# A spectral filter and a Gelu feed-forward block on one core: where the filter tables come from, and when batch 1 is transformed

## The chip, the cores and the metric

The kernel runs on one core of a Trainium2 chip. The metric is the device time of one execution in microseconds; before the change it is 802.97 us, the median of three runs (802.93 to 803.73). The profile is one execution, with a span of 798.2 us.

The engines are named as in the profile: PE is TensorE (matmuls; PEld are its weight loads), DVE is VectorE, ACT is ScalarE, POOL is GpSimd, SP is SyncE, whose queue issues transfers. SBUF is the memory beside the engines, with 128 partitions; PSUM holds the results of matmuls, and DRAM is outside the core.

## The reference

`x` has 8 batches of 3008 positions with 256 channels. Along the positions it is transformed (a real Fourier transform), multiplied with a complex filter for each frequency and channel, and transformed back. The result goes through a feed-forward block with an exact Gelu:

```python
X = np.fft.rfft(x, axis=1)                 # x: (8, 3008, 256)
F = (filt_r + 1j * filt_i)[None, :, :]     # (1505, 256), two real tables
y = np.fft.irfft(X * F, n=3008, axis=1)
h = y.reshape(24064, 256) @ w_in           # (256, 2048)
g = 0.5 * h * (1 + erf(h / sqrt(2)))
out = g @ w_out                            # (2048, 256)
```

Inputs and output are float32; the kernel works in bfloat16 with float32 sums.

## The kernel before

3008 is 47 x 64, and the transform is done in two steps by matmuls with small tables: T1 over the 47, T2 over the 64; then the filter, then T3 and T4 back. Batches 1 to 7 go through four kinds of units: `s1` (first step, 16 units of one matmul, line 233), `s2` (second step and filter, 12 units, line 256), `s3` (back, 12 units, line 280), `s4` (back, 16 units, line 307). Between `s1` and `s2`, and between `s3` and `s4`, the data must change their layout, which they do by being written to DRAM (`R1`, `R2`) and read back (`r1`, `r2`). Batch 0 has nothing to hide behind, and is done in its own way without DRAM (`c1`, `c1t`, `c2`, `c3`, `c3t`), with transposes on PE.

The filters lie in `F`: both tables, 24 rows of 256 channels, in four groups of 32 partitions. Groups 0 and 1 hold a direct and a mirrored reading of the table; groups 2 and 3 hold the same again, for the other half of each complex product. Before the change the lower half is read from DRAM (with a cast from float32) and the upper half is copied from it:

```python
    def load_filters(self, k0, k):
        nc, D = self.nc, self.D
        for t, src in enumerate((self.filt_r, self.filt_i)):
            direct = _dram(src, k0 * D, [[NA * D, 32], [D, k], [1, D]])
            mirror = _dram(src, (NA - k0) * D, [[NA * D, 32], [-D, k], [1, D]])
            for q, a in enumerate((direct, mirror)):
                nc.gpsimd.dma_start(out=self.F[32 * q:32 * q + 32, t, k0:k0 + k, :], in_=a)
        nc.sync.dma_start(out=self.F[64:128, :, k0:k0 + k, :], in_=self.F[0:64, :, k0:k0 + k, :])
```

The filter product of batch 0; a step `p` uses rows 2p and 2p+1 of F:

```python
    def c2(self, p):
        # ...
        for t, o, n in ((p1, 1, 0), (p2, 0, 1)):
            # ... two matmuls (line 350) with T2[:, k, o:o + 2] into ps
            nc.vector.tensor_tensor(out=t, in0=ps, op=ALU.mult,                    # line 353
                                    in1=self.F[:, n, 2 * p:2 * p + 2, :].rearrange("p a b -> p (a b)"))
```

The table T2 has three parts: 1 and 2 come from Sin activations on ScalarE, and part 0, which only `c2` of batch 0 uses, is the negative of part 2 (the sign copy). At the end of `table_2_sin`:

```python
        act(out=self.T2[:, :, 2, 32:64], in_=self.a2[:, :, 32:64], func=AF.Sin, scale=2.0 * PI, bias=self.hm)
        self.nc.vector.tensor_scalar(out=self.T2[:, :, 0, :], in0=self.T2[:, :, 2, :], scalar1=-1.0, scalar2=None,
                                     op0=ALU.mult)
```

The order of the start-up, cut:

```python
    # ... x of batch 0 in 8 loads, tables T1 and T2
    for k in range(0, K1, 6):
        m.load_filters(k, 6)
    m.load_w_in()
    for u in range(16):
        m.c1(u // 2, u % 2)
        if u == 8:
            m.table_2_sin()
    m.load_x(1)
    m.load_w_out(0)
    m.load_w_out(8)
    m.tables_inverse()           # T3, T4 by matmuls, cast by ScalarE and VectorE
    warm = g.tile([128, 1], FP32, name="warm")
    nc.scalar.activation(out=warm, in_=m.p, func=AF.Gelu)    # loads the Gelu table
    for p in range(14):
        if p < 12:
            m.c1t(p)             # transpose, copied out by ScalarE (line 340)
        if 1 <= p < 13:
            m.c2(p - 1)
        if p in (3, 5, 7, 9, 11, 13):
            m.c3((p - 3) // 2)
    # ... c3t and s4 of batch 0
```

After that the kernel is a row of slots. In slot s, `mm1` makes one of 16 column blocks of the hidden layer for 512 tokens (two matmuls, line 408, and a Gelu on ScalarE, line 411), and from slot 16 on `mm2` makes a quarter of an output tile (four matmuls, line 422). The units of the next batch are put into slots; `s1, n1` give the slot of the first unit and the slots from one to the next, and so on. `s3` follows `s2` by 4 slots. The tokens of batch 1 are needed from slot 80:

```python
    for b in range(1, B):
        hi = first(b)            # (b * S // 512) * 16
        if b == 1:
            s1, n1, r1, s2, n2, r2, s4, n4 = 0, 0.5, 8, 17, 3.2, 58, 66, 0.8
        else:
            s1, n1, r1, s2, n2, r2, s4, n4 = hi - 94, 1, hi - 78, hi - 69, 3.7, hi - 23, hi - 17, 1
        for u in range(16):
            put(s1 + int(u * n1), m.s1, b, u)
            put(s4 + int(u * n4), m.s4, b, u // 2, u % 2)
        for c in range(4):
            put(r1, m.r1, b, c)
            put(r2, m.r2, b, c)
        for p in range(12):
            put(s2 + int(n2 * p), m.s2, b, p)
            put(s2 + int(n2 * p) + 4, m.s3, b, p)
        # ... loads of the batch after it
```

Of the kernel before, what the change touches and what calls it, by code (L numbers as in the profile page):

```python
# [9 lines left out]
AF = mybir.ActivationFunctionType  # L10
ALU = mybir.AluOpType
# [7 lines left out]
K1 = 24  # L19
# [5 lines left out]
def _dram(src, off, dims):  # L25
    return dataclasses.replace(src, offset=src.offset + off, ap=[list(d) for d in dims])


class _Mix:
# [59 lines left out]
    def load_filters(self, k0, k):  # L89
        nc, D = self.nc, self.D  # L90
        for t, src in enumerate((self.filt_r, self.filt_i)):
            direct = _dram(src, k0 * D, [[NA * D, 32], [D, k], [1, D]])
            mirror = _dram(src, (NA - k0) * D, [[NA * D, 32], [-D, k], [1, D]])
            for q, a in enumerate((direct, mirror)):
                nc.gpsimd.dma_start(out=self.F[32 * q:32 * q + 32, t, k0:k0 + k, :], in_=a)
        nc.sync.dma_start(out=self.F[64:128, :, k0:k0 + k, :], in_=self.F[0:64, :, k0:k0 + k, :])

    def gate(self, t):

# [80 lines left out]
    def table_2_sin(self):  # L180
        act = self.nc.scalar.activation
        act(out=self.T2[:, :, 1, :], in_=self.w2, func=AF.Sin, scale=2.0 * PI)
        act(out=self.T2[:, :, 2, 0:32], in_=self.a2[:, :, 0:32], func=AF.Sin, scale=-2.0 * PI, bias=self.hp)
        act(out=self.T2[:, :, 2, 32:64], in_=self.a2[:, :, 32:64], func=AF.Sin, scale=2.0 * PI, bias=self.hm)
        self.nc.vector.tensor_scalar(out=self.T2[:, :, 0, :], in0=self.T2[:, :, 2, :], scalar1=-1.0, scalar2=None,
                                     op0=ALU.mult)

    def tables_inverse(self):

        nc = self.nc  # L190
        for t4, t1, wt in ((self.T4, self.T1p, self.wt), (self.T4c, self.T1q, self.wtc)):
            ps = self.bank("ps_t4", wide=True)
            nc.tensor.matmul(ps[0:96, 0:2 * NA], lhsT=t1.rearrange("p a b c -> p (a b c)"),
                             rhs=self.eye[0:2 * NA, 0:2 * NA], start=True, stop=True)
            nc.vector.tensor_scalar(out=t4.rearrange("p n h -> p h n"),
                                    in0=ps[0:96, 0:2 * NA].rearrange("p (h n) -> p h n", h=2),
                                    scalar1=wt[0:96], scalar2=None, op0=ALU.mult)
        for q in range(6):
            ps = self.bank("ps_t3", wide=True)
            for i in range(4):  # L200
                nc.tensor.matmul(ps[:, 128 * i:128 * i + 128],
                                 lhsT=self.T2[:, 4 * q + i, 1:3].rearrange("p a b -> p (a b)"),
                                 rhs=self.eye, start=True, stop=True)

            self._evac(self.T3[:, 4 * q:4 * q + 4], ps.rearrange("p (k n r) -> p k r n", k=4, r=2), True)
# [225 lines left out]
@with_exitstack  # L431
def kernel(
    ctx: ExitStack,
    tc: tile.TileContext,
    x: bass.AP,
    filt_r: bass.AP,
    filt_i: bass.AP,
    moe_w_in: bass.AP,
    moe_w_out: bass.AP,
    out: bass.AP,  # L440
):
    m = _Mix(ctx, tc, x, filt_r, filt_i, moe_w_in, moe_w_out, out)
    nc, B, S = tc.nc, m.B, m.S
    NT = B * S // TCH
    ctx.enter_context(tc.manual_schedule())

    g = m.small
    m.p = m.iota(g, "p", [128, 1], [[0, 1]], cm=1)
    m.load_x(0, 0, 1)
    m.table_1(g)  # L450
    m.T1c = g.tile([2 * NA, 96], BF16, name="T1c")
    nc.vector.tensor_copy(out=m.T1c.rearrange("p (k h r) -> p k h r", h=2, r=2),
                          in_=m.T1.rearrange("p (h r k) -> p k h r", h=2, r=2))
    m.load_x(0, 1, 2)
    m.pi = m.iota(g, "pi", [128, 1], [[0, 1]], cm=1, dt=I32)
    m.kap = m.py.tile([128, K1, 2 * NB], FP32, tag="y", name="kap")[:, :, 0:NB]
    for sgn, lo in ((1, 0), (-1, 32)):
        nc.gpsimd.iota(m.kap[:, :, lo:lo + 32], pattern=[[1, K1], [sgn * NA, 32]], base=min(0, sgn * NA),
                       channel_multiplier=0, allow_small_or_imprecise_dtypes=True)
    m.table_2(g)  # L460
    m.load_x(0, 2, 4)
    cols = m.iota(g, "cols", [128, 128], [[1, 128]])
    m.eye = g.tile([128, 128], BF16, name="eye")
    nc.vector.tensor_scalar(out=m.eye, in0=cols, scalar1=m.p, scalar2=None, op0=ALU.is_equal)
    m.T1p = g.tile([2 * NA, 2, K1, 2], BF16, name="T1p")
    nc.vector.tensor_copy(out=m.T1p, in_=m.T1.rearrange("p (h r k) -> p h k r", h=2, r=2))
    m.T1q = g.tile([2 * NA, K1, 2, 2], BF16, name="T1q")
    nc.vector.tensor_copy(out=m.T1q, in_=m.T1.rearrange("p (h r k) -> p k r h", h=2, r=2))
    for k in range(0, K1, 6):
        m.load_filters(k, 6)  # L470
    m.load_w_in()


# [6 lines that stand above are left out]
    m.load_w_out(8)  # L480
    m.tables_inverse()
    warm = g.tile([128, 1], FP32, name="warm")
    nc.scalar.activation(out=warm, in_=m.p, func=AF.Gelu)
    for p in range(14):
        if p < 12:
            m.c1t(p)
        if 1 <= p < 13:
            m.c2(p - 1)
        if p in (3, 5, 7, 9, 11, 13):
            m.c3((p - 3) // 2)  # L490
    for u in range(20):
        if u < 16:
            m.c3t(u)
        if u >= 3 and u % 2 == 1 and (u - 3) // 2 < 8:
            for h in range(2):
                m.s4(0, (u - 3) // 2, h, both=True)


    at = {}

    def put(slot, f, *a):
        at.setdefault(slot, []).append((f, a))

    def first(b):
        return (b * S // TCH) * 16

    for b in range(1, B):
        hi = first(b)
        if b == 1:
            s1, n1, r1, s2, n2, r2, s4, n4 = 0, 0.5, 8, 17, 3.2, 58, 66, 0.8  # L510
        else:
            s1, n1, r1, s2, n2, r2, s4, n4 = hi - 94, 1, hi - 78, hi - 69, 3.7, hi - 23, hi - 17, 1
        for u in range(16):
# [8 lines that stand above are left out]
        if b + 1 < B:  # L522
            for i in range(8):
                put(s2 + int(n2 * (i + 2)), m.load_next, b, i + 2, i // 2, i % 2)

    for s in range((NT + 1) * 16):
        t, jc = s // 16, s % 16
        for f, a in at.pop(s, ()):
            f(*a)
        if t >= 1:  # L530
            m.mm2(t - 1, jc)
        if t < NT:
            m.mm1(t, jc)
    assert not at
# [30 lines left out]
```

## Time and profile before

| What | Value |
|---|---|
| time, median of three runs | 802.97 us |
| span of the profiled run | 798.2 us |
| PE busy | 767.3 us, 96% |
| ACT busy | 569.6 us, 71% |
| DVE busy | 406.4 us, 51% |
| `mm1`, one Gelu (line 411) | 752 of 597 ns |
| casts of `s1` (line 220, a_sb) | 112 of 684 ns |
| filter copies inside SBUF | 4 of 384 KB, 7.8 us to landing (median) |
| filter loads from DRAM | 16 of 96 KB as written, 5.9 us to landing (median) |

Durations of single instructions overlap with those of the next one on the same engine, so a row of Gelus runs at a shorter interval than 597 ns. Busy shares are averages over stages that have different limits; what counts for a change in one stage is which wait ends last there. The profile's views that are used below are the chain that ended last (in order of time), the timeline (instructions in order, with idle time and what ended it in brackets), and the busy time by stretches.

### The profile page before, as it was taken

The numbers are of one execution on the slowest core, as the hardware profiler recorded it, in microseconds if no ns is written. First come the engines' busy times: TensorE is split into PE (matmuls) and PEld (weight loads), VectorE is DVE, ScalarE is ACT, GpSimd is POOL, SyncE is SP. The second block draws the span as 40 slices with busy tenths as digits, with TensorE's granted clock in tenths as the row PEclk, the third lists the DMA queues.
The fourth block names the chain that finished last, engine by engine and source line by source line (L and its number), as shares of the span: only waits on it lengthen the run. The fifth ranks groups of instructions, "written<-read, shape, count | busy, mean of one in ns | idle before, by whom it ended". The sixth has DMA issues, their size and how long they took to land.

```text
span 798.2 us, 14871 instructions
## 1 busy us (share of the span) xinstructions
PE 767.3 (96%) x5950; PEld 547.5 (69%) x6042; DVE 406.4 (51%) x733; ACT 569.6 (71%) x982; POOL 56.6 (7%) x145
## 2 busy tenths in 40 slices
PE   4788999999999999999999999999999999999998
PEld 4654767667676766767677676777667776676666
DVE  6793745466453764546456464555645366420111
ACT  6667975598656885578855887558865689566663
POOL 8300200011000110002000020001100000000000
PEclk9999999999999999999999999999999999999999
DMA  8953761546425554345534466154661512401111
GB/s 140 234 100 106 147 160 47 158 109 125 128 69 156 107 104 134 77 154 109 132 85 109 139 130 146 46 134 124 118 153 54 172 62 72 133 27 40 41 41 53
DMA packets 86918, 87.23 MB, mean 109 GB/s; under 512 B 5888, under 2 KB 76544, under 8 KB 86848
## 3 DMA queue, kind: packets, MB, share of 16 engines
q1 hardware_dynamic: 78336, 70.27, 30.7%
q0 software_dynamic: 8512, 16.00, 13.8%
q8 instruction: 47, 0.77, 0.4%
q14 instruction: 23, 0.19, 0.1%
HBM read 54.00 MB, written 46.66 MB: 126 GB/s over the span
## 4 chain that ended last, share of the span: by engine, by line
PE 89%; DMA 5%; DVE 3%; issue 1%; POOL 1%; ACT 0%; SPq 0%; DVEq 0%; POOLq 0%
PE ps_o L422 41%; PE ps_h L408 37%; PE ps_s L307 3%; PE ps_s L233 3%; PE ps_s L256 2%; PE ps_s L280 2%; DMA d_sb<-R 2%; DMA x_sb<-in_x_dram 2%; DVE a_sb L220 1%; DVE d_sb L220 1%; POOL x_sb L87 1%; DVE p L353 0%; DMA b_sb<-R 0%; DVE y_sb L222 0%; DMA R<-a_sb 0%
## 5 line engine op out<-in xcount | busy, mean ns | idle before, releaser
L411 ACT ACTIVATE g_sb<-ps_h 128x512 bf16<-128x512 f32 x752 | 438.5, 597 | 194.7 <-PE ps_h L408 171.2
L422 PE MATMUL ps_o<-w_out_sb,g_sb 128*128 128x256 bf16 x3008 | 449.9, 273 | 2.6
L408 PE MATMUL ps_h<-y_sb,w_in_sb 128*128 128x512 bf16 (+7 forms) x1636 | 427.9, 350 | 0.1
L422 PEld LDWEIGHTS <-g_sb 128*128 128x128 bf16 x3008 | 287.9, 98 | 128.7 <-issue 0.6
L408 PEld LDWEIGHTS <-w_in_sb 128*128 128x128 bf16 x1728 | 165.0, 98 | 29.8 <-issue 3.9
L426 DVE COPY ost<-ps_o 128x512 f32<-128x512 f32 x94 | 64.3, 684 | 122.4 <-PE ps_o L422 121.9
L263 DVE TENSOR_TENSOR p<-ps_s,F 128x512 bf16<-128x512 f32 x84 | 58.1, 692 | 115.1 <-ACT p L262 109.0
L222 DVE TENSOR_SCALAR y_sb<-ps_s 128x376 bf16<-128x376 f32 x120 | 65.4, 547 | 81.6 <-PE ps_s L307 81.5
L220 DVE CAST a_sb<-ps_s 96x512 bf16<-96x512 f32 x112 | 75.5, 684 | 40.9 <-PE ps_s L233 40.9
L220 DVE CAST v_sb<-ps_s 128x512 bf16<-128x512 f32 x84 | 57.6, 686 | 13.0 <-PE ps_s L280 13.0
L307 PEld LDWEIGHTS <-d_sb 96*128 96x128 bf16 x512 | 34.0, 97 | 30.8 <-DMA d_sb<-R 3.9
L261 ACT ACTIVATE p<-ps_s 64x512 bf16<-64x512 f32 x84 | 49.8, 593 | 5.3 <-PE ps_s L256 3.3
L262 ACT CAST p<-ps_s 64x512 bf16<-64x512 f32 x84 | 48.5, 577 | 1.0
L233 PE MATMUL ps_s<-x_sb,T 94*96 94x512 bf16 x112 | 42.7, 383 | 1.3 <-DVE a_sb L220 1.0
L101 POOL COPY gate<-p 1x1 bf16<-1x1 bf16 x48 | 8.5, 176 | 494.4 <-DVE p L265 494.4
L307 PE MATMUL ps_s<-T,d_sb 96*128 96x94 bf16 x448 | 36.6, 204 | 2.7 <-DMA d_sb<-R 1.5
L265 DVE TENSOR_TENSOR p<-p,p 128x512 bf16<-128x512 bf16 x84 | 35.7, 425 | 2.9
L256 PE MATMUL ps_s<-b_sb,T 128*128 128x256 bf16 x168 | 32.1, 273 | 4.0 <-DMA b_sb<-R 3.6
L87 POOL DMA_DIRECT2D x_sb<-in_x_dram x64 | 33.8, 530 | 20.9 <-issue 11.6
L264 DVE TENSOR_TENSOR p<-p,F 128x512 bf16<-128x512 bf16 x84 | 34.9, 415 | 0.0
L280 PE MATMUL ps_s<-p,T 128*128 128x256 bf16 x168 | 32.1, 273 | 0.4
L280 PEld LDWEIGHTS <-T 128*128 128x128 bf16 x168 | 16.4, 98 | 19.8
(84 smaller groups left out, 182.6 us busy)
## 6 DMA issues: line engine op xcount, KB each, us to landing
out_dram<-ost SPq DMA_DIRECT2D x94, 256.0 KB, 2.5
x_sb<-in_x_dram POOLq DMA_DIRECT2D x64, 188.0 KB, 4.0
R<-a_sb SPq DMA_DIRECT2D x56, 192.0 KB, 3.0
b_sb<-R SPq DMA_DIRECT2D x28, 384.0 KB, 4.3
R<-v_sb SPq DMA_DIRECT2D x42, 256.0 KB, 4.0
d_sb<-R SPq DMA_DIRECT2D x56, 192.0 KB, 4.5
F<-F SPq DMA_DIRECT2D x4, 384.0 KB, 7.8
w_in_sb<-in_moe_w_in_dram POOLq DMA_DIRECT2D x2, 512.0 KB, 10.1
```

What stands on the lines that cost most here:

```text
L220: self.nc.vector.tensor_copy(out=out, in_=in_)
L222: self.nc.vector.tensor_scalar(out=out, in0=in_, scalar1=scale, scalar2=None, op0=ALU.mult)
L233: nc.tensor.matmul(ps[0:96, :], lhsT=self.T1, rhs=self.st[b, "x"][:, 2 * u:2 * u + 2, :], start=True, stop=True)
L261: nc.scalar.activation(out=p2[0:64], in_=ps[64:128], func=AF.Copy, scale=-1.0)
L262: nc.scalar.copy(out=p2[64:128], in_=ps[0:64])
L263: nc.vector.tensor_tensor(out=p1, in0=ps, in1=f(0), op=ALU.mult)
L280: nc.tensor.matmul(ps[:, 256 * i:256 * i + 256], lhsT=self.T3[:, k].rearrange("p a b -> p (a b)"), rhs=w[:, 256 * i:256 * i + 256], start= ...
L307: nc.tensor.matmul(ps[:, 94 * i:94 * i + 94], lhsT=d[:, (grp % 2) * 4 + i, 128 * half:128 * half + 128], rhs=t4, start=True, stop=True)
L408: nc.tensor.matmul(ps[:, o:o + n], lhsT=self.w_in_sb[:, dc, jc * 128:jc * 128 + 128], rhs=self.y[b][:, dc, off:off + n], start=(dc == 0), ...
L411: nc.scalar.activation(out=self.st["g", t][:, jc, :], in_=ps, func=AF.Gelu)
L422: nc.tensor.matmul(ps[:, tile_i % 2, :], lhsT=g[:, jc, tile_i * 128:tile_i * 128 + 128], rhs=self.w_out_sb[:, jc, :], start=(jc == 0), sto ...
L426: nc.vector.tensor_copy(out=ost, in_=ps)
```

## The change

It has four parts. (1) Both halves of F are read from DRAM, so the copy inside SBUF goes; a part is then complete as soon as its loads have landed, instead of after loads and copy. (2) The parts have 4, 6, 6 and 8 rows instead of 6 each, so that the first one is small. (3) The Gelu table is loaded in the course of the batch 0 steps instead of ahead of them, and the sign copy stands after the casts of the first step on VectorE instead of between them. (4) The units of batch 1 are placed anew: one `s1` unit in each slot instead of two in each of the first eight, the read `r1` at slot 16 instead of 8, the first `s2` at slot 26 instead of 17 with 2.8 slots between them instead of 3.2, `r2` at 61 and `s4` from 68.

```diff
-            for q, a in enumerate((direct, mirror)):
+            for q, a in enumerate((direct, mirror, direct, mirror)):
                 nc.gpsimd.dma_start(out=self.F[32 * q:32 * q + 32, t, k0:k0 + k, :], in_=a)
-        nc.sync.dma_start(out=self.F[64:128, :, k0:k0 + k, :], in_=self.F[0:64, :, k0:k0 + k, :])
@@ table_2_sin, tables_inverse
-        self.nc.vector.tensor_scalar(out=self.T2[:, :, 0, :], in0=self.T2[:, :, 2, :], scalar1=-1.0, scalar2=None,
-                                     op0=ALU.mult)
     def tables_inverse(self):
         nc = self.nc
+        nc.vector.tensor_scalar(out=self.T2[:, :, 0, :], in0=self.T2[:, :, 2, :], scalar1=-1.0, scalar2=None,
+                                op0=ALU.mult)
@@ start-up
-    for k in range(0, K1, 6):
-        m.load_filters(k, 6)
+    for k, n in ((0, 4), (4, 6), (10, 6), (16, 8)):
+        m.load_filters(k, n)
@@
-    nc.scalar.activation(out=warm, in_=m.p, func=AF.Gelu)
     for p in range(14):
         # ... c1t(p), c2(p - 1)
+        if p == 4:
+            nc.scalar.activation(out=warm, in_=m.p, func=AF.Gelu)
@@ slots
-            s1, n1, r1, s2, n2, r2, s4, n4 = 0, 0.5, 8, 17, 3.2, 58, 66, 0.8
+            s1, n1, r1, s2, n2, r2, s4, n4 = 0, 1, 16, 26, 2.8, 61, 68, 0.72
```

## The prediction

> **What bounds the kernel now.** I read the page first: busy time, the chain that ended last, the groups. TensorE (PE) is busy for 96% of the 798.2 us span and carries most of the chain:
>
> ```profile
> PE 767.3 (96%) x5950; PEld 547.5 (69%) x6042; DVE 406.4 (51%) x733; ACT 569.6 (71%) x982; POOL 56.6 (7%) x145
> ...
> PE 89%; DMA 5%; DVE 3%; issue 1%; POOL 1%; ACT 0%; SPq 0%; DVEq 0%; POOLq 0%
> ```
>
> The change removes no matmul, so it can only gain where PE is not the limit. To find those places I read the same chain in order of time (start us, us, what), then the timeline there (start, length, engine and line, and in brackets the idle time before it and what ended that).
>
> ```profile
> 8.37 6.14 DMA x_sb<-in_x_dram
> ...
> 19.15 1.28 ACT L483
> ...
> 50.40 9.57 DVE a_sb L220 x16
> 60.34 3.16 DMA R<-a_sb
> 63.82 3.36 DMA b_sb<-R
> ```
>
> Beyond 70 us the chain is PE almost without a break. So there are two stretches to look at.
>
> Start-up, up to 50.2 us, when the first matmul of the feed-forward part (L408) runs:
>
> ```profile
> 20.56 1.05 ACT L340 CAST b_sb<-ps_c1t 128x512 bf16<-128x512 f32 x2
> ...
> 23.01 6.30 DVE L353 TENSOR_TENSOR p<-ps_c,F 128x512 bf16<-128x512 f32 x10 [3.00 <-DMA F<-F]
> ...
> 31.63 3.68 DVE L353 TENSOR_TENSOR p<-ps_c,F 128x512 bf16<-128x512 f32 x6 [0.83 <-DMA F<-F]
> ```
>
> The first filter product waits 3.00 us for the copy of the filters inside SBUF, and the third part costs another 0.83 us. The Gelu table load (L483 in the chain) stands ahead of the copy of the first transposed block (20.56), but the filters come later still.
>
> First feed-forward tiles, 50.2 to 75 us:
>
> ```profile
> 50.32 9.64 DVE L220 CAST a_sb<-ps_s 96x512 bf16<-96x512 f32 x16
> ...
> 59.07 4.51 ACT L411 ACTIVATE g_sb<-ps_h 128x512 bf16<-128x512 f32 x9 [0.60 <-PE ps_h L408]
> ...
> 67.23 0.39 PE L256 MATMUL ps_s<-b_sb,T 128*128 128x256 bf16 x2 [3.60 <-DMA b_sb<-R]
> ```
>
> In slots 0 to 7 two transform units of batch 1 go between single feed-forward units, and VectorE needs 9.64 us for their 16 casts (0.60 each). In slots 8 to 15 ScalarE sets the pace, 4.51/9 = 0.50 us per Gelu. Then PE stands still for 3.60 us, because slot 17 asks for batch 1's data before they have gone through DRAM. What follows is seen in the table by stretch of 1 us (PE, weight load, DVE, ACT, POOL busy; then granted clock, DMA share, GB/s):
>
> ```profile
> 66.00:67.00 1.00, 0.00 (x0) 0.00 (x0) 0.00 (x0) 0.00 (x0) 0.00 (x0) 1.00 1.02 378
> ...
> 69.00:70.00 1.00, 1.00 (x5) 0.39 (x4) 0.97 (x3) 0.46 (x1) 0.00 (x0) 0.50 0.46 173
> 70.00:71.00 1.00, 1.00 (x6) 0.71 (x5) 0.35 (x1) 0.60 (x1) 0.00 (x0) 0.50 0.00 0
> ```
>
> After the gap the clock is granted at half, from about 68.3 to 71.7 us.
>
> [...] 3.60 us idle, then about 3.4 us near 0.50. [...] in this trace the DMA share is 0.85 or more from 3 to 45 us. [...] the filters are f32 in DRAM and bf16 in SBUF, and the loads stand on POOL's queue here. [...] The trace shows the 1.28 us, and the next activation 0.02 us later[...]; I take 1.28 plus about 0.15 for the one-column activation.
>
> **The change part by part.**
>
> *1. Batch 1 units moved (the largest part).* Costs of one unit on PE, from starts in the timeline of PE: feed-forward input and output 0.435 us each (both, 130.70 to 131.57), forward unit (L233) 0.22 (134.42 to 134.65), filter units L256 and L280 0.22 each, inverse unit (L307) 0.17. After the change one forward unit goes into each of slots 0 to 15. A slot then needs PE 0.435 + 0.22 = 0.655, VectorE 0.60, ScalarE 0.50: PE-bound, 16 x 0.655 = 10.5 us. Before, the first output matmul starts at 62.60, so the 16 slots took 12.4. Saved: **1.9 us**.
>
> The wait. Before, the last cast ends at 59.96 and PE resumes at 67.2, so write, read and latency take 7.25 us. After, counted from the first feed-forward matmul: last cast at about 15 x 0.655 + 0.4 + 0.7 = 10.9, data there at 18.2. The first use is now slot 26, at 10.5 + 10 x 0.87 = 19.2. The wait of **3.6 us** goes, with 1.0 us to spare. With it goes the half clock: 3.4 to 3.6 us at half speed lose about **1.8 us**.
>
> Cross-check: slots 0 to 79 took from 50.2 to 132.0 us (the first 128x448 tile of L408 is slot 80), 81.8 us. The work of PE after the change is 10.5 + 64 x 0.87 + 12 x 0.44 + 16 x 0.17 = 74.2, a difference of 7.6; the three terms give 7.3.
>
> What is given back: filter units come every 2.8 slots instead of 3.2. ScalarE then needs 2.8 x 0.50 + 1.17 = 2.6 us in 2.8 x 0.87 + 0.44 = 2.9 of PE, so PE still leads, but chains get tighter; I take 0.4 us. Between the last filter unit (slot 60) and the first inverse unit (68) lie 8 slots instead of 10. Batch 2 already has 8 and there PE waits 0.31 us at 209.68. I take 0.3. Net of part 1: **-6.6 us**.
>
> *2. Filters.* Four copies of 384 KB inside SBUF (1.57 MB) go, sixteen more casting loads from DRAM (1.57 MB as written) come. While only loads run, 3 to 17 us, the rate is 125 to 177 GB/s, mean 158 over the stretches of 2 us. First batch plus all filters are 1.54 + 3.15 = 4.69 MB: 29.7 us from 3.0, so the last filter part lands near **32.7**. By the same count parts 1 to 3 land near 16, 21 and 26. A POOL issue takes about 0.53 us, and each waits for the load eight before it to land; two of part 1 wait until 13.87 and 14.80 as now, and 3.7 us to landing gives 18.5 for part 1.
>
> *3. Table load and sign copy.* With the table load gone from ahead of it, the first block's copy starts at about 19.7, its matmuls at 20.3, the first product at **20.7** instead of 23.01. The sign copy (0.56 us of VectorE) merely trades places with four casts; their sum ends near 20.0 either way, and I give it nothing. From 20.7 on, two products take 2.7 us per pair of steps where nothing is late (the copies into vt_sb start at 28.63 and 31.32), so 12 steps take 16.2, and the table load, now inside a ScalarE chain with some slack, costs about 1.0: the products end at 37.9. From the filters: last part at 32.7, 4 steps of 1.23 (two 0.61 products) and 0.3 of latency, 37.9 too. Now they end at 39.5. Net of parts 2 and 3: **-1.6 us**. Stages after it are unchanged up to the first feed-forward matmul, then at about 48.6. Behind the filters come w_in, batch 1 and w_out, 3.63 MB at about 190 GB/s (the rate after 36 us): batch 1 complete near 46.5, w_out near 52. Both are in time, w_out being used from slot 16.
>
> Sum: 802.97 - 6.6 - 1.6 = **794.8 us**.
>
> **Rivals.** *Bandwidth takes the place of the copy.* For it: the engines are full until 45 us, and 1.57 MB more from DRAM cost some 10 us of them at 158 GB/s, while the copies that go were moved beside the loads (206 to 272 GB/s from 23 to 33 us). If the last part lands at 35 or later, the products end at 40 and start-up loses 0.5 us or more, total 797. Against it: what is late then (batch 1, w_out) has slack. *The wait in DRAM comes back in part.* The margin is 1.0 us; a slower write would leave a wait of 1 to 2 us[...]: 796 to 797. *The tighter schedule binds.* If 2.8 slots make ScalarE or VectorE the bound, 12 units lose perhaps 0.2 us each: 797. *Everything better*: products without stalls and no cost of the table load: 792.
>
> **Range and chances.** The loss in the DRAM wait and the clock is read straight from the trace, so the sign is near certain. Start-up can be off by 2 us, the schedule by 1.5. Range 791.8 to 798.4. A change of 2% would be 16 us, more than both stretches can give. Faster by over 2%: 0.02; within: 0.96; slower: 0.02.
>
> **What would show it.** Right: no wait of L256 on b_sb over 0.5 us near 67 us and a clock of 1.00 from 60 to 75; 16 slots in 10.5 to 11.5 us; first filter product near 20.7 with no wait on F, last product ending near 38; slot 80 about 74 to 75.5 us after the first L408. Wrong: a wait of a product on F over 2 us near 32 us, a wait of L307 on d_sb over 1 us before slot 80, or a forward unit waiting on batch 1's load.

## The result and the profile after

The changed kernel takes 792.44 us (median of four runs, 792.14 to 793.09) against 802.95 (801.68 to 803.73): a ratio of 0.9872, 95% interval 0.9855 to 0.9889, or 10.5 us less. The prediction was 794.8, with a range of 791.8 to 798.4. The profiled span went from 798.2 to 790.4 us, only 7.8 us less; where the other 2.7 us are is one of the questions below.

The first part and the chain of the page of the changed kernel (its lines are numbered one less from the filter load on):

```profile
PE 762.5 (96%) x5950; PEld 545.3 (69%) x6042; DVE 407.4 (52%) x733; ACT 570.1 (72%) x982; POOL 65.3 (8%) x161
...
PE 90%; DMA 4%; POOL 2%; DVE 2%; issue 1%; ACT 0%; SPq 0%; DVEq 0%; POOLq 0%
```

DMA and VectorE lost a point each of the chain, POOL gained one. The timeline from the first feed-forward matmul on (start us, length, what, in brackets the idle time before and what ended it):

```profile
49.25 0.61 PE L407 MATMUL ps_h<-y_sb,w_in_sb 128*128 128x512 bf16 x2 [0.18 <-ACT y_sb L217]
49.35 10.58 DVE L219 CAST a_sb<-ps_s 96x512 bf16<-96x512 f32 x16
49.90 10.37 ACT L410 ACTIVATE g_sb<-ps_h 128x512 bf16<-128x512 f32 x16 [0.70 <-PE ps_h L407]
59.48 0.60 PE L421 MATMUL ps_o<-w_out_sb,g_sb 128*128 128x256 bf16 x4
...
68.16 0.38 PE L255 MATMUL ps_s<-b_sb,T 128*128 128x256 bf16 x2
...
123.65 0.60 PE L407 MATMUL ps_h<-y_sb,w_in_sb 128*128 128x448 bf16 x4
```

The same places in the kernel before:

```profile
50.22 0.61 PE L408 MATMUL ps_h<-y_sb,w_in_sb 128*128 128x512 bf16 x2
...
62.60 0.60 PE L422 MATMUL ps_o<-w_out_sb,g_sb 128*128 128x256 bf16 x4
...
132.01 0.60 PE L408 MATMUL ps_h<-y_sb,w_in_sb 128*128 128x448 bf16 x4
```

The 16 slots with one forward unit each take 10.23 us (49.25 to 59.48, where the first output matmul starts) instead of 12.4. The first use of batch 1's data, at 68.16, has no idle time in brackets, so nothing is waited for. Slots 0 to 79 take 74.40 us (49.25 to 123.65) instead of 81.79. The stretches of 1 us show the clock at 1.00 where it was at 0.50:

```profile
69.00:70.00 1.00, 0.95 (x7) 0.69 (x7) 0.00 (x0) 0.99 (x2) 0.00 (x0) 1.00 0.96 365
70.00:71.00 1.00, 1.00 (x10) 0.70 (x8) 0.81 (x2) 0.98 (x3) 0.00 (x0) 1.00 0.57 203
```

The start-up is 0.97 us shorter (first feed-forward matmul at 49.25 instead of 50.22). Its products, in the timeline:

```profile
19.79 3.08 DVE L352 TENSOR_TENSOR p<-ps_c,F 128x512 bf16<-128x512 f32 x5 [0.45 <-PE ps_c L349]
...
28.35 3.90 DVE L352 TENSOR_TENSOR p<-ps_c,F 128x512 bf16<-128x512 f32 x6 [0.71 <-DMA F<-in_filt_i_dram]
...
34.29 4.28 DVE L352 TENSOR_TENSOR p<-ps_c,F 128x512 bf16<-128x512 f32 x7 [2.03 <-PE ps_c L349]
```

The first one starts 3.2 us earlier than before. At step 8, before its second product, VectorE is idle for 2.03 us again. The bracket names PE, but this is a wait for several semaphores, of which the last by the profile is named; the chain in order of time shows what it was:

```profile
14.75 6.14 POOL F L95 x11
21.09 2.58 POOL F L95 x5
23.79 4.45 DMA F<-in_filt_i_dram
28.52 5.66 DMA F<-in_filt_i_dram
```

The last filter load is issued at 28.52 and lands at 34.18; the product starts 0.11 us later. Ahead of it the chain is GpSimd issuing loads.

### The profile page after: what moved, and what is told of

Same layout as the page of the kernel before. It is cut to its first block, busy times and chain, and to the rows that moved or that the text cites. A ratio compares the mean times of both kernels' runs of the same rounds, so it can differ in the third digit from the quotient of the medians.

```text
span 790.4 us, 14879 instructions
## 1 busy us (share of the span) xinstructions
PE 762.5 (96%) x5950; PEld 545.3 (69%) x6042; DVE 407.4 (52%) x733; ACT 570.1 (72%) x982; POOL 65.3 (8%) x161
## 4 chain that ended last, share of the span: by engine, by line
PE 90%; DMA 4%; POOL 2%; DVE 2%; issue 1%; ACT 0%; SPq 0%; DVEq 0%; POOLq 0%
PE ps_o L421 41%; PE ps_h L407 37%; PE ps_s L232 3%; PE ps_s L306 3%; PE ps_s L279 2%; PE ps_s L255 2%; DMA d_sb<-R 2%; DMA F<-in_filt_i_dram 1%; POOL F L95 1%; DMA x_sb<-in_x_dram 1%; DVE d_sb L219 1%; POOL x_sb L87 1%; DVE p L352 0%; DVE y_sb L221 0%; POOL kap L457 0%
```

## Experiments: batch 1 units, wait and clock

These four kernels ran on one chip, where the kernel before took 801.5 us (median of 29 runs).

**The placement alone.** The kernel before with the one line of slots replaced:

```diff
-            s1, n1, r1, s2, n2, r2, s4, n4 = 0, 0.5, 8, 17, 3.2, 58, 66, 0.8
+            s1, n1, r1, s2, n2, r2, s4, n4 = 0, 1, 16, 26, 2.8, 61, 68, 0.72
```

> The kernel before with the new placement of batch 1 alone. The profiles say that slots 0 to 79 shrink from 81.8 to 74.4 us, so 7.4 us less; the medians differ by 10.5 us, the profiled spans by 7.8. Theory A (wait and half clock after it carry the change, and the half clock lasts longer in most executions than in the profiled one): 8.5 to 10 us less than before, near 793.5. Theory B (the part that the profile doesn't show lies in the start-up's transfers): 7.4 us less, near 795.5.

Measured: 793.64 us, 7.9 less; ratio 0.9901 (0.9881 to 0.9921). Slots 0 to 79 take 74.57 us in its profile. The placement brings most of the change. It fell short of the 8.5 of theory A by less than its interval, and lies as near to the 7.4 of theory B; alone it doesn't separate the two.

**The start-up alone.** The changed kernel with the old line of slots.

> The changed kernel with the old placement of batch 1: filters, table load and sign copy alone. Theory A: first feed-forward matmul 1.0 us earlier, as in the profile of the changed kernel, and 0.5 to 1.5 us less in all, with the wait for b_sb of 3 to 4 us and the half clock still there. Theory B: 2.5 to 3.5 us less.

Measured: 800.1 us, 1.4 less; ratio 0.9985 (0.9973 to 0.9997). The first feed-forward matmul is at 48.85, 1.4 us earlier than in the profile of the kernel before. Theory B is out: the part that the first profiles didn't show isn't in the start-up. The 1.4 and the 7.9 add up to 9.3; the changed kernel, run again beside a kernel before of 802.18, had 9.3.

Its profiled execution shows something more. The waits from 45 us on (who for whom, us in total, times, longest) and then the table of stretches:

```profile
PE ps_s L255 <- DMA b_sb<-R: 3.3, 1, 3.3
```

```profile
66.00:68.00 2.00, 1.95 (x16) 1.41 (x16) 0.77 (x2) 1.95 (x4) 0.00 (x0) 1.00 0.84 312
68.00:70.00 2.00, 2.00 (x17) 1.42 (x15) 0.68 (x2) 1.69 (x4) 0.00 (x0) 1.00 0.09 33
70.00:72.00 2.00, 2.00 (x16) 1.42 (x15) 1.51 (x4) 1.85 (x4) 0.00 (x0) 1.00 0.00 0
```

PE stood still for 3.3 us, and the clock stayed at 1.00. This execution took 796.72 us, the shortest of 22, whose median is 800.1. So the half clock doesn't follow each time, and the profiled execution of a kernel with such a gap needn't be a typical one. The granted clock of each run says the same of one and the same kernel: over the 29 runs of the kernel before it goes from 0.993 to 1.000, and the two runs at 1.000 are the two shortest (796.96 and 797.65 us). Its profiled execution took 799.96 us, 3.0 less than the median of 802.95; that of the changed kernel took 792.14, 0.3 less than its median. That is where the other 2.7 us are.

**The wait and the half clock away, the pace kept.** The kernel before with

```diff
-            s1, n1, r1, s2, n2, r2, s4, n4 = 0, 0.5, 8, 17, 3.2, 58, 66, 0.8
+            s1, n1, r1, s2, n2, r2, s4, n4 = 0, 0.5, 8, 22, 2.9, 58, 66, 0.8
```

> The kernel before, with only the first s2 at slot 22 instead of 17 and 2.9 slots between them; s1 stays at two in a slot. This takes the wait away without the other pace. Theory A: no wait over 0.5 us on b_sb and the clock at 1.00 from 60 to 80 us; the wait of 3.6 and the half clock go, 5 to 8 us less, with 1.9 left to the pace. Theory C (the wait only moves, since the data come no earlier and other work runs out): under 2 us less.

Measured: 795.54 us, 6.0 less; ratio 0.9922 (0.9905 to 0.9939). The first use, at 68.69, waits for nothing and the clock stays at 1.00. Theory C is out. What the full placement has beyond this, 7.9 - 6.0 = 1.9 us, is what the pace was predicted to bring (1.9). Each of the two medians is known to some 1.5 us only; but the profiles agree, with 76.37 us for slots 0 to 79 here and 74.57 with the full placement, 1.8 less.

**The clock alone.** The kernel before with matmuls that nobody reads, in the gap:

```diff
+        if b == 1:
+            put(17, m.warm_up, 15)      # 15 matmuls 128x512 of w_in with itself
         for u in range(16):
```

> The kernel before with 15 matmuls of 128x512 whose result nobody reads, put into slot 17 ahead of the first s2: some 3.3 us of work for TensorE in the wait. The data come no earlier. Theory A: the clock stays at 1.00 and 1.5 to 5 us go, the same as the half clock costs. Theory C or B (the half clock costs nothing that counts): same time as before, or up to 0.5 us more.

Measured: 797.98 us, 3.5 less; ratio 0.9958 (0.9941 to 0.9976). The timeline of PE and two of the stretches:

```profile
63.57 3.40 PE L211 MATMUL ps_warm<-w_in_sb 128*128 128x512 bf16 x14
67.33 0.39 PE L256 MATMUL ps_s<-b_sb,T 128*128 128x256 bf16 x2 [0.36 <-DMA b_sb<-R]
```

```profile
68.00:69.00 1.00, 1.00 (x9) 0.69 (x7) 0.03 (x1) 0.96 (x3) 0.00 (x0) 1.00 0.95 375
69.00:70.00 1.00, 1.00 (x9) 0.64 (x7) 1.00 (x2) 1.00 (x2) 0.00 (x0) 1.00 0.97 375
```

The data come at the same time as in the kernel before (67.33 and 67.23), so the wait for them is all there; only the clock differs. More work in the gap makes the kernel faster, and the half clock costs 3.5 us in the median of executions (1.9 to 4.7 by the interval), against the 1.8 of the execution that the prediction read. The granted clocks point the same way with a smaller size: their mean is 0.9967 over the 29 runs of the kernel before, an estimated 2.6 us of lost work ((1 - 0.9967) x 801), and 0.9991 over the eight runs here, 0.7 us, so an estimated 1.9 us for the filled gap. How much more than 1.8 it is isn't settled. The runs also lie closer: 796.9 to 799.7, where those of the kernel before went from 797.0 to 804.9.

## Experiments: filters, table load and sign copy

The changed kernel ran again beside three that undo one part of it.

> The changed kernel itself once more, to stand beside the three that undo one part of it: 792 to 793 us, the first feed-forward matmul at 49.0 to 49.5 us.

Measured: 792.90 us (792.12 to 793.58); ratio 0.9888 (0.9865 to 0.9910); first feed-forward matmul at 49.48.

**The filters as before** (two loads for each table and part, then the copy; parts of 6 rows).

> The changed kernel with the filters as before: four parts of 6 rows, upper half copied inside SBUF. Theory A (the DRAM reads gain by bringing the first part early, since the first product no longer waits for load and copy): first product near 22 us instead of 19.8, first feed-forward matmul at 50 to 51, 0.8 to 1.5 us longer than the changed kernel. Theory D (the last part, late by the transfers added, gives all of it back): within 0.3 us of the changed kernel.

Measured: 794.29 us, 1.4 more than the changed kernel beside it; ratio 0.9908 (0.9884 to 0.9931). The timeline of VectorE:

```profile
22.70 3.68 DVE L353 TENSOR_TENSOR p<-ps_c,F 128x512 bf16<-128x512 f32 x6 [3.31 <-DMA F<-F]
...
35.86 3.76 DVE L353 TENSOR_TENSOR p<-ps_c,F 128x512 bf16<-128x512 f32 x6 [0.21 <-PE ps_c L350]
```

Theory A holds against theory D: the first product waits 3.31 us for its copy and starts 2 us later than in the changed kernel beside it (20.71). But after that no product waits for filters any more; the changed kernel gives back part of its lead at its last filter part. Two things differ here, the copy and the sizes of the parts. Four equal parts read from DRAM, tried below, take 10.5 us less than the kernel before beside them, these copied ones 7.9 less than theirs, so the copy itself costs more than the 1.4 (about 2.6, across two chips).

The wait for the copy was also followed by half clock in this execution, from 25.3 to 28.7 us. PE's timeline and one stretch (the clock is the third number from the end):

```profile
23.45 0.23 PE L367 MATMUL ps_c<-T,p 128*128 128x128 bf16 x1 [1.80 <-DVE p L353]
24.04 0.34 PE L367 MATMUL ps_c<-T,p 128*128 128x128 bf16 x3 [0.37 <-DVE p L353]
```

```profile
26.00:28.00 2.00, 2.00 (x18) 1.75 (x16) 0.90 (x2) 1.71 (x4) 0.75 (x2) 0.50 1.02 221
```

No single wait of PE there was longer than 1.80 us. What this half clock costs was not measured.

**The table load ahead** of the batch 0 steps again.

> The changed kernel with the Gelu table loaded ahead of the batch 0 steps, as before. Theory A: the first product moves from 19.8 to about 21.2 us (1.28 of table load and 0.15), and since the last part of the filters at 34.2 sets the end of the products, the time changes by less than 0.5 us. Theory E (ScalarE's chain sets the start-up): 1.0 to 1.5 us longer.

Measured: 793.50 us, 0.6 more; the first product at 21.83, the first feed-forward matmul at 49.21, no later than in the changed kernel (49.48). Theory E is out; the move of the table load alone brings nothing that these runs can tell from zero, since the last filter part (34.26 here) sets the end of the products either way.

**The sign copy back** among the casts.

> The changed kernel with the sign copy back among the casts of the first step. The prediction gave its move nothing; the traces show that VectorE's casts of T3 end at 19.34 after the change and 20.0 before it, because the copy stood waiting for ScalarE with ready casts behind it. Theory A: these casts end 0.6 to 0.7 us later again, the first product near 20.5, and the end changes by less than 0.5 us because the last filter part sets it. Theory E: 0.6 us longer.

Measured: 794.74 us, with runs from 792.8 to 797.6; the median is 1.8 us above the changed kernel beside it, more than either theory gave. What the copy does to VectorE is plain in the timelines. The kernel before:

```profile
15.35 0.56 DVE L185 TENSOR_SCALAR T<-T 128x1536 bf16<-128x1536 bf16 x1 [2.51 <-ACT T L184]
15.83 1.94 DVE L220 CAST at_sb<-ps_c 128x384 bf16<-128x384 f32 x4
...
18.14 1.87 DVE L220 CAST T<-ps_t 128x512 bf16<-128x512 f32 x3
```

The changed kernel:

```profile
12.27 1.47 DVE L219 CAST at_sb<-ps_c 128x384 bf16<-128x384 f32 x3
15.44 1.20 DVE L219 CAST at_sb<-ps_c 128x384 bf16<-128x384 f32 x2 [1.69 <-PE ps_c L322]
16.55 0.55 DVE L188 TENSOR_SCALAR T<-T 128x1536 bf16<-128x1536 bf16 x1
...
17.47 1.87 DVE L219 CAST T<-ps_t 128x512 bf16<-128x512 f32 x3
```

The copy waited 2.51 us for ScalarE's Sin with two casts behind it whose inputs were there; after the change these run at 12.27, and the casts of T3 start 0.7 us earlier. With the copy put back the casts of T3 start at 17.85, between the two, and the first product at 20.72, just as in the changed kernel beside it (20.71). Whether the move shortens the whole isn't settled: in this profiled execution the last filter part also came late (35.6 instead of 34.5), which the copy doesn't explain.

**The late last part.** Three more kernels vary the filter loads, and one more followed from them; all ran on one chip with a kernel before of 800.7 to 801.1 us. First, nothing beside the last loads: GpSimd reads one element of the last one before it issues w_in.

> The changed kernel with one element of the last filter load read on GpSimd ahead of the load of w_in, so that nothing runs beside the last filter loads. If these share the DMA engines with w_in and that is what makes them late: they land near 32.5 instead of 34.2 and the kernel takes 1 to 1.5 us less. If the issues on GpSimd set the time (the last one at 28.5): under 0.5 us less, and the loads behind them move back by 4 us, in time for their use.

Measured: 793.28 us (791.4 to 795.3); ratio 0.9905 (0.9888 to 0.9923). POOL's timeline, then VectorE's:

```profile
27.12 2.13 POOL L95 DMA_DIRECT2D F<-in_filt_i_dram  x4
34.20 0.18 POOL L109 COPY gate_f<-F 1x1 bf16<-1x1 bf16 x1 [4.95 <-DMA F<-in_filt_i_dram]
```

```profile
34.19 4.27 DVE L354 TENSOR_TENSOR p<-ps_c,F 128x512 bf16<-128x512 f32 x7 [1.80 <-DMA F<-in_filt_i_dram]
```

The last part lands at 34.2, as without the hold. So the traffic behind it isn't what makes it late. GpSimd issues until 29.25, nearly without a pause from 15.5 on, and 5 us later the data are there. For most of these 5 us the DMA engines are still full (the last two numbers are the mean busy share of the 16 engines and GB/s):

```profile
29.00:31.00 2.00, 1.91 (x30) 1.74 (x28) 1.83 (x4) 1.39 (x3) 0.25 (x1) 1.00 1.11 158
31.00:33.00 2.00, 1.77 (x27) 1.70 (x26) 1.39 (x3) 1.36 (x4) 0.00 (x0) 1.00 1.16 183
```

So transfers had piled up behind the issues, and at the end it is the moving of bytes that takes the time. That faster issues alone would hardly have brought the last part earlier follows from this, but no run shows it.

Second, fewer loads: rows 10 to 23 copied inside SBUF, rows 0 to 9 still read twice.

> The changed kernel with rows 0 to 9 read twice from DRAM and rows 10 to 23 copied inside SBUF again: 8 of 32 casting loads go, two copies come on another queue. If the late last part (34.2 us) is what holds up the start-up, and it comes from 32 issues of 0.53 us on GpSimd's queue plus the bytes: the last products start 1 to 2 us earlier, 1 to 2 us less than the changed kernel, about 791. If a copy takes as long as in the kernel before (8 to 9.5 us to landing beside other loads): no gain or up to 1 us longer.

Measured: 800.02 us; ratio 0.9988 (0.9980 to 0.9996), nearly all of the gain lost, and neither expectation met: the kernel is about 7 us longer than the changed kernel.

```profile
23.51 3.08 DVE L354 TENSOR_TENSOR p<-ps_c,F 128x512 bf16<-128x512 f32 x5 [0.78 <-PE ps_c L351]
34.83 2.48 DVE L354 TENSOR_TENSOR p<-ps_c,F 128x512 bf16<-128x512 f32 x4 [8.24 <-DMA F<-F]
```

A copy takes 9 to 10 us to land beside the loads of w_in and batch 1, which GpSimd now issues earlier (w_in at 24.3 instead of 29.1). The products wait 8.24 us, the clock drops in this stretch too (0.88 from 20 to 35 us, 0.78 to 50), and the first feed-forward matmul is at 56.63. The copy is slow just where its data are awaited. This mixture is worse than copies throughout. A likely reason is that the third part's copy is issued at 25.59 here, after more loads from DRAM, and at 22.99 there; no run tests it.

Third, the sizes: four parts of 6 rows.

> The changed kernel with four parts of 6 rows instead of 4, 6, 6 and 8; same bytes, same number of loads. Theory A (total of bytes or issues sets the last part): the first part lands 1 to 2 us later, the last part's last load at 34 again, but it is needed only from step 9 instead of 8, so the time is the same within 0.5 us. If the small first part is what counts: 0.7 to 1.5 us longer than the changed kernel at 792.4 to 792.9.

Measured: 790.61 us (790.12 to 792.5); ratio 0.9875 (0.9862 to 0.9889). Neither expectation: it is faster. The first feed-forward matmul is 1.7 us earlier than in the changed kernel:

```profile
47.52 0.61 PE L407 MATMUL ps_h<-y_sb,w_in_sb 128*128 128x512 bf16 x2 [0.19 <-ACT y_sb L217]
```

Hence a last one, with the sizes reversed:

```diff
-    for k, n in ((0, 4), (4, 6), (10, 6), (16, 8)):
+    for k, n in ((0, 8), (8, 6), (14, 6), (20, 4)):
```

> The changed kernel with the parts in the reverse order of size: 8, 6, 6 and 4 rows; same bytes, same number of loads. With 4, 6, 6, 8 the last part stops the products by about 2 us at step 8; with equal parts it is needed from step 9 and no wait for it is left. Theory F (the last part is what counts: it lands at the same time whatever its size, so the later the step that needs it the better): no wait of a product on F after 27 us, first feed-forward matmul at 47.3 to 48.3 us, 790 to 791.5 us, like equal parts. Theory G (the small first part is what brings the gain): first product 1.5 us or more later than 20.7 and the start-up no shorter than in the changed kernel, 792.5 or more.

Measured: 790.84 us (790.3 to 791.35); ratio 0.9871 (0.9849 to 0.9893). The timeline of VectorE:

```profile
20.48 6.33 DVE L352 TENSOR_TENSOR p<-ps_c,F 128x512 bf16<-128x512 f32 x10 [0.55 <-PE ps_c L349]
...
33.12 3.76 DVE L352 TENSOR_TENSOR p<-ps_c,F 128x512 bf16<-128x512 f32 x6 [0.21 <-PE ps_c L349]
```

and, for the end of the start-up, PE's first feed-forward matmul:

```profile
47.56 0.61 PE L407 MATMUL ps_h<-y_sb,w_in_sb 128*128 128x512 bf16 x2 [0.19 <-ACT y_sb L217]
```

Theory F: even with the largest part first the first product doesn't wait for filters, and with the smallest last no later one does. The products end at 36.88 instead of 38.57. In the two executions of the changed kernel that were profiled, the first product starts at 19.79 and 20.71, so a small first part buys little, and a large last one costs about 1.7 us. Both variants have ten runs between them, nine of them at 791.4 or less; the changed kernel's ten runs start at 792.1. But they ran on different chips, and against the kernel before beside each, the gains can't be told apart (10.5 and 9.9 for the variants, 10.5 and 9.3 for the changed kernel). On the variants' chip the changed kernel ran only with w_in held, at 793.28. So the 1.7 us rest on the profiles: 47.52 and 47.56 for the first feed-forward matmul, against 48.85 to 49.48 in four executions with the changed kernel's parts (the changed kernel twice, with the old placement, and with w_in held).

## Why the prediction was right, point by point

The time of 792.44 us lies in the range, 2.3 below the 794.8. In terms of the change, 8.2 us were predicted, 10.5 measured, and 9.3 when both kernels ran again; so about half of the 2.3 didn't come again.

**Pace of slots 0 to 15.** Predicted 10.5 us, measured 10.23; the saving was to be 1.9, the profiles have 2.15 (12.38 - 10.23), and the medians of the two placements differ by 1.9. Right.

**Wait.** Predicted to go, with 1.0 us to spare. It went. The read was issued at 64.06; in the kernel before the data came 3.4 us after the issue, which gives 67.5 for a use at 68.16, an estimate of 0.7 us to spare.

**Half clock.** That it goes with the wait was right, but the size was read from one execution: 1.8 us, where filling the gap was worth 3.5 in the median (1.9 to 4.7) and an estimated 1.9 by the granted clocks. Runs of one and the same kernel differ: the kernel before has granted clocks from 0.993 to 1.000 and times over 8 us (796.96 to 804.91), against 1.5 for the changed kernel (792.12 to 793.58). What decides whether a gap is followed by half clock, these runs don't show: the gap of 3.3 us was not, the one of 3.6 was. And the prediction's rival that left a wait of 1 to 2 us (796 to 797) counted no half clock; in the start-up with the copies back, a wait of 1.80 us with shorter ones after it was followed by half clock.

**Given back.** Predicted 0.4 for the tighter filter units and 0.3 for the inverse units. Slots 0 to 79 take 74.40 us; PE's work there, with the measured 10.23 for the first 16 slots instead of 10.5, is an estimated 73.9. So about 0.5 for both, against 0.7, and no wait of PE is listed from 66 to 125 us.

**First product.** Predicted 20.7, measured 19.79 and 20.71. Right. The sign copy was given nothing, because the sum of VectorE's work stays the same. That overlooked that the copy was waiting with ready work behind it: 0.7 us on VectorE. But that these 0.7 us reach the first product isn't shown.

**Last filter part.** Predicted 32.7 by bytes, measured 34.18. The term that was mis-sized is the rate: 4.69 MB from 3.0 to 34.18 us are 150 GB/s, not the 158 of the stretch before 17 us. GpSimd's issues, 24 of them from 15.29 to 29.09, 0.575 each, left hardly a pause either (the last had waited 0.46 us, until the load eight before it, issued at 23.79, had landed at 28.24), and every kernel here with fewer loads also moves fewer bytes, so no run separates the two fully. One of the prediction's own signs of being wrong came true, a wait of a product on F over 2 us (2.03, at 34.29), and the rival "bandwidth takes the place of the copy" came in part: the products ended at 38.57 instead of 37.9.

**Start-up as a whole.** Predicted to gain 1.6. The two profiles give 1.0 and the medians 1.4. That it comes so near, with the last part 1.5 us late, is partly luck: the old start-up was on average longer than in the one profile that the prediction read. Its first feed-forward matmul is at 50.22 there and at 51.29, 51.11 and 50.33 in three other kernels with the same start-up (mean 50.74); with the new start-up it is at 49.25, 48.85 and 49.48 (mean 49.19).

**Later loads.** Batch 1 and w_out were in time, as predicted; no forward unit waits for them.

## What to carry to other kernels

A wait of TensorE can cost more than its own length: after the gap of 3.6 us here, the half clock cost an estimated 1.9 to 3.5 us more, and not in each execution. Look at several runs' times and granted clocks, and price the clock by filling the gap with matmuls that nobody reads. When transfers stream in by parts while a chain consumes them, look at the last part and the step that needs it: here four equal parts and a small last part both took the wait away (2.03 us) that a large last part had left. An instruction that waits can hold up ready work behind it for longer than it takes itself: the sign copy, 0.56 us on VectorE, stood waiting for 2.51 us with two ready casts behind it. Whether that reaches the end is another question, to be asked of the wait that ends last.

## What the runs showed of the hardware that was not expected

- PE idle for 3.3 us with no loss of clock after it in one execution (796.72 us, median of the same kernel 800.1), and for 3.6 us with 3.4 us at half clock in another kernel's. Half clock for 3.4 us also (25.3 to 28.7 us, the kernel with the filters copied) after a stretch in which PE worked 0.8 us of 3.6 (21.65 to 25.24) but never waited longer than 1.80 us at a time.
- Casting loads of 64 to 128 KB were issued by GpSimd about every 0.5 to 0.6 us whatever their size; at 0.53 us each, 32 of them are an estimated 17 us of its queue.
- Copies inside SBUF took long to land beside loads from DRAM: 7.8 us in the median for the four of 384 KB in the kernel before, 9.1 and 10.0 us for one of 384 and one of 512 KB in the kernel with rows 10 to 23 copied.
